# Retention, soft mixture and top-2 mixture on one core: a token table laid out by partition, and expert one's row list made from its own 24 columns

## The chip, the cores and the metric

One core of one Trainium2 chip. The metric is the device time of one execution, in microseconds. Three runs of the kernel before took 586.41, 589.7 and 592.46 us, so the median is 589.7.

## The reference, cut to what matters

```python
y = retention(q, k, v)                      # B, H, S, D = 4, 8, 768, 64
x = y.transpose(0, 2, 1, 3).reshape(3072, 512)
logits = x @ phi                            # soft mixture: 32 slots, 4 for each of 8 experts
d = softmax(logits, axis=0)                 # each slot over all tokens
slot_out = [relu((d.T @ x)[e] @ w1[e]) @ w2[e] for e in range(8)]
c = softmax(logits, axis=1)                 # each token over the 32 slots
x = c @ slot_out
noisy = x @ w_gate + log1p(exp(x @ w_noise)) * noise
top2 = two largest of noisy for each token, with their softmax as weights
for e in range(8):                          # w1: 512 x 1024, w2: 1024 x 512
    rows = tokens with e among their top2
    out[rows] += weight[rows] * (relu(x[rows] @ w1[e]) @ w2[e])
```

## The kernel before, in words

The first 195 us or so compute the retention and the soft mixture's slots. Its result `x` is never stored. A token's row of `x` is its 32 combine weights times the slot outputs, so for the second mixture the kernel keeps a small DRAM table, `ctab`: for each of the 3072 tokens 32 combine weights (`cs`, made in combine(), L561 to 577) and 8 gate weights (`wsl`, L689 to 692), 40 numbers of 4 bytes, in the order of the tokens, and a row of zeros behind them (L175). A hidden row of expert e is then the token's 32 weights times `gs` of e, which is the slot outputs times w1[e], made by g_dot(e) (`pg`), rounded into two parts (`gr`) and spread over the partitions (`gs`), by matmul for expert 0 (g_rep, L726) and by 16 small transfers on SyncE's queue for the others (g_copy, L737).

Gating (L633 to 692): on VectorE the two largest entries are picked (`sel`), `selh` marks both, and two steps of matmuls (`pt`, `pp`) count, for each token and expert, the token's place in the expert's list. `blk` (L676) is the block of 128 that the place lies in, `rr` (L677) the place within the block, for all 8 experts × 24 chunks of tokens = 192 columns; `cnt` (L679, ScalarE) the experts' counts. While VectorE and GpSimd do that, TensorE runs dummy matmuls (fill, tile `pw`; F4 of them before g_dot(0), L638).

lists(e) (L750) makes the list of an expert: `bm` (VectorE, which block), `bt` (GpSimd, `bm` times two constants, "base" for the chunk and "tok" for the token), `oh` (VectorE, 3 compares of `tab` with `rr`), `pli` (TensorE, 24 small matmuls), and `lt` and `ls` (VectorE), the token numbers. Expert 0 and 1 have lists of their own; lists_all() (L774) makes those of the other six together, in pieces that are resumed after the output blocks in PACED (L958 ff.): `bma`, `rk`, `rs` and `rh` after block (0, 1), `oh` after (0, 2), `sb` (GpSimd, L804) and `bta` (VectorE, L807) after (0, 3), and the same again for the second choice after (0, 4), (0, 5) and (1, 0). A piece is tied to its block by a mark, a copy of one element of the block's `yo` on ScalarE into the tile that the piece will write.

The experts: fetch() (L845) gathers table rows by the list (GpSimd, an indirect DMA for each block, `cg`), turn() (L855) rounds and transposes them (`cts`, `st` on ScalarE and VectorE, `ptc` on TensorE, `cts` again), hidden() (L895) multiplies by `gs` (`phc`) and makes both parts of the result (`hhl`: L907 on ScalarE, L909 and L912 on VectorE), and main() (L921) multiplies by w2 in three passes (`pyc`, 24 matmuls for a block of 128 rows), scales to `yo` on ScalarE, and add_rows() (L917) scatters `yo` to `out` from GpSimd by the same list `ls`, adding up. An expert has 7 blocks, six of 128 rows and one of 64; more than that goes to a loop at the end that is not entered here. Weights w1 and w2 (`V1`, `V2`) come by SyncE's queue; ScalarE and VectorE split V2 into `wh` and `wl`. load_paced (L963) ties a piece of a weight to a block by a mark like the ones above (L957), and SyncE issues its transfers in the order of the program. The order on each engine is set by a scheduler that keeps the order of the source, adds the edges of after(), and moves what it can.

Of the kernel before, what the change touches and what calls it, by code (L numbers as in the profile page):

```python
# [105 lines left out]
def kernel(ctx: ExitStack, tc: tile.TileContext, q, k, v, phi, w1, w2,  # L106
# [641 lines left out]
    LS = {}  # L748

    def lists(e, pool, ps, nb):  # L750
        rv = rr.rearrange("p (e c) -> p e c", e=E)
        bv = blk.rearrange("p (c e) -> p c e", e=E)
        bm = pool.tile([P, NCH, nb], F16, name="bm", bufs=1)
        nc.vector.tensor_tensor(bm, bv[:, :, e:e + 1].to_broadcast([P, NCH, nb]),
                                col16("iotab")[:, None, :nb].to_broadcast([P, NCH, nb]), op=OP.is_equal)
        bt = pool.tile([P, NCH, 2, nb], F16, name="bt", bufs=1)
        nc.gpsimd.tensor_tensor(bt[:, :, 0, :], bm, col16("base")[:, :, None].to_broadcast([P, NCH, nb]), op=OP.mult)
        nc.gpsimd.tensor_tensor(bt[:, :, 1, :], bm, col16("tok")[:, :, None].to_broadcast([P, NCH, nb]), op=OP.mult)
        oh = pool.tile([P, NCH // 8, P, 8], F16, name="oh", bufs=1)
        for c in range(NCH // 8):  # L760
            nc.vector.tensor_tensor(oh[:, c], tab, rv[:, e, None, 8 * c:8 * c + 8].to_broadcast([P, P, 8]),
                                    op=OP.is_equal)
        pl = ps.tile([P, 2, nb], F32, name="pli", tag="pt")
        for c in range(NCH):
# [354 lines left out]
```

## Time and profile before

| what | value |
|---|---|
| median of 3 runs | 589.7 us |
| profiled execution, its own time | 592.0 us |
| its span | 590.2 us |
| TensorE busy | 554.7 us, 94% of the span |
| VectorE, ScalarE, GpSimd busy | 43%, 41%, 38% |
| mean granted clock of TensorE | 0.964 |

The profiled execution took 2.3 us more than the median, and 1.8 us of it lie outside the span. The clock row of the page is full (9 of 10 or more) in nearly all slices behind the fifteenth, which is the stretch from about 215 us on.

### The profile page before, as it was taken

The page shows a single profiled execution, that of the slowest core. Times are in us where ns is not written, and L with a number is a line of the kernel's source. Part 1 is how long each engine was busy: PE and PEld are TensorE (multiplying, and loading weights), DVE is VectorE, ACT ScalarE, POOL GpSimd, SP SyncE. Part 2 cuts the span into 40 slices and gives each one's busy share as a digit, 9 for nine tenths or more (in the row PEclk, how much of TensorE's full clock was granted, in tenths as well). Part 3 has the DMA queues.
Part 4 walks back from the last instruction along what each step waited for, and adds up shares of the span by engine and source line. Part 5 has one row for each costly group of instructions (what it writes and reads, how often), then busy time and mean ns, then how long its engine had stood idle before and what let it go on. Part 6 is the DMA issues. An engine that isn't in the chain of part 4 may idle for free. (4 is left out here: it accounts for less than half of the span.)

```text
span 590.2 us, 10723 instructions
## 1 busy us (share of the span) xinstructions
PE 554.7 (94%) x4196; PEld 421.8 (71%) x4196; DVE 255.3 (43%) x529; ACT 243.7 (41%) x543; POOL 222.5 (38%) x214
## 2 busy tenths in 40 slices
PE   7999999999899878979999999999999999999990
PEld 4787888787443436858787787787787787788880
DVE  3566777764202366456625235235235234334200
ACT  2555656553101235245246246246345335335210
POOL 3524534330103055642455444344344436332231
PEclk7899999999699789989999999999999999999997
DMA  9999999998799942465446646656656644553232
GB/s 218 286 270 306 299 328 281 308 405 364 291 404 389 367 124 67 102 179 151 108 98 182 125 132 186 124 151 168 137 140 170 143 112 65 132 105 46 37 43 31
DMA packets 79485, 111.76 MB, mean 189 GB/s; under 512 B 10066, under 2 KB 51602, under 8 KB 78530
## 3 DMA queue, kind: packets, MB, share of 16 engines
q1 hardware_dynamic: 65808, 95.96, 49.3%
q0 software_dynamic: 9696, 14.37, 16.7%
q10 hardware_dynamic: 3922, 0.66, 0.6%
q8 instruction: 35, 0.57, 0.4%
q14 instruction: 24, 0.20, 0.1%
HBM read 87.92 MB, written 20.41 MB: 184 GB/s over the span
## 5 line engine op out<-in xcount | busy, mean ns | idle before, releaser
L937 PE MATMUL pyc<-wh,hhl 128*128 128x512 f32 x384 | 154.6, 403 | 0.2 <-ACT hhl L907 0.2
L938 PE MATMUL pyc<-wl,hhl 128*128 128x512 f32 x384 | 152.1, 396 | 0.0
L939 PE MATMUL pyc<-wh,hhl 128*128 128x512 f32 x384 | 151.5, 395 | 0.0
L918 POOL DMA_INDIRECT out_dram<-yo,lsa x42 | 66.1, 1575 | 136.1 <-ACT w L957 31.6
L909 DVE SCALAR_TENSOR_TENSOR hhl<-phc,hhl 128x512 fp32r<-128x512 f32 (+1 forms) x128 | 66.9, 551 | 84.9 <-ACT hhl L907 84.5
L939 PEld LDWEIGHTS pyc<-wh,hhl 128*128 128x128 f32 x384 | 72.6, 189 | 16.6
L937 PEld LDWEIGHTS pyc<-wh,hhl 128*128 128x128 f32 x384 | 72.1, 188 | 16.1 <-ACT hhl L907 0.4
L946 ACT ACTIVATE yo<-pyc,cg 128x512 f32<-128x512 f32 x48 | 33.0, 688 | 121.0 <-PE pyc L939 108.1
L938 PEld LDWEIGHTS pyc<-wl,hhl 128*128 128x128 f32 x384 | 72.4, 189 | 14.6
L907 ACT ACTIVATE hhl<-phc 128x512 fp32r<-128x512 f32 (+1 forms) x128 | 59.5, 513 | 8.0 <-PE phc L904 6.6
L885 DVE TENSOR_TENSOR wl<-w,wh 128x1024 fp32r<-128x1024 f32 x32 | 39.1, 1225 | 49.6 <-ACT wh L879 49.6
L851 POOL DMA_INDIRECT cg<-ctab,lsa x42 | 43.8, 1042 | 15.2 <-issue 14.9
L879 ACT CAST wh<-w 128x1024 fp32r<-128x1024 f32 x32 | 33.4, 1047 | 32.3 <-DMA w<-in_moe_w_dram 24.7
L298 DVE TENSOR_TENSOR am<-pa,cta 128x512 f32<-128x512 f32 x48 | 33.1, 692 | 28.6 <-PE py L322 15.3
L918 POOL DMA_INDIRECT out_dram<-yo,ls x14 | 25.0, 1787 | 47.4 <-ACT w L957 16.2
L256 POOL TENSOR_TENSOR comp<-raws,cta 64x512 f32<-64x512 f32 x24 | 24.9, 1039 | 40.7 <-PE py L322 16.5
L276 DVE TENSOR_TENSOR qT<-pt,cta 64x512 f32<-64x512 f32 x48 | 33.0, 688 | 16.6 <-PE pt L271 16.2
L256 POOL TENSOR_TENSOR vl<-raws,cta 64x512 f32<-64x512 f32 x24 | 24.9, 1038 | 33.5 <-PE py L322 22.6
L904 PE MATMUL phc<-cts,gs 128*128 128x256 f32 (+1 forms) x192 | 36.5, 299 | 0.5 <-ACT cts L873 0.5
L904 PEld LDWEIGHTS phc<-cts,gs 128*128 128x128 f32 x192 | 29.8, 191 | 7.3 <-issue 2.5
L294 PE MATMUL pa<-qT,kT 64*128 64x128 f32 x384 | 31.7, 296 | 0.7 <-DVE qT L276 0.7
L294 PEld LDWEIGHTS pa<-qT,kT 64*128 64x128 f32 x384 | 27.0, 198 | 5.2 <-issue 3.7
(195 smaller groups left out, 701.6 us busy)
## 6 DMA issues: line engine op xcount, KB each, us to landing
w<-in_moe_w_dram SPq DMA_DIRECT2D x80, 512.0 KB, 5.1
w<-in_moe_w_dram SPq DMA_DIRECT2D x11, 2048.0 KB, 10.5
comp<-in_q_dram SPq DMA_DIRECT2D x12, 512.0 KB, 6.7
out_dram<-zt SPq DMA_DIRECT2D x6, 1024.0 KB, 9.8
raws<-in_k_dram SPq DMA_DIRECT2D x11, 512.0 KB, 5.6
raws<-in_v_dram SPq DMA_DIRECT2D x11, 512.0 KB, 7.8
gs<-gr SPq DMA_DIRECT2D x112, 32.0 KB, 2.3
w<-in_moe_w_dram SPq DMA_DIRECT2D x2, 1024.0 KB, 21.1
```

Source lines behind the costliest of these rows:

```text
L256: pool_ins[0] = nc.gpsimd.tensor_tensor(VL[j][rs], RAW[u][1][gs, :, r, :], gv[gs, r, t, :, None].to_broadcast([64, H, D]), op=OP.mult)
L294: mm = nc.tensor.matmul(pa[s][:, hp, :], KT[j][r, hp, :], QT[t][r, hp, g, :], start=True, stop=True)
L851: nc.gpsimd.indirect_dma_start(out=cg[:rows(b), i, :], out_offset=None, in_=ctab, in_offset=index(e, b, rows(b)))
L879: ins = nc.scalar.copy(wh, V2[e][:, 1024 * i:1024 * i + 1024])
L885: nc.vector.tensor_tensor(wl, V2[e][:, 1024 * i:1024 * i + 1024], WH[e][i], op=OP.subtract)
L904: nc.tensor.matmul(ph[:, w * i:w * i + w], GS[e][:, kf + i], CT[e, g][:, :w], start=True, stop=True)
L907: relu.append(nc.scalar.activation(h[:, :, :w], pv, AF.Relu))
L909: last = nc.vector.scalar_tensor_tensor(h[:, :, w + t0:w + t0 + 2 * P], pv[:, :, :2 * P], 0.0, h[:, :, :2 * P], op0=OP.max, op1=OP.subtract)
L918: nc.gpsimd.indirect_dma_start(out=out, out_offset=index(e, b, n), in_=y, in_offset=None, bounds_check=N - 1, oob_is_err=False, compute_op ...
L937: nc.tensor.matmul(py, hhl[:, kf, ts], wh, start=(kf == 0), stop=False)
L938: nc.tensor.matmul(py, hhl[:, kf, ts], wl, start=False, stop=False)
L939: nc.tensor.matmul(py, hhl[:, kf, tl], wh, start=False, stop=(kf == KF - 1))
```

## The change

- **Table.** `ctab` is laid out by partition: row p·24 + c holds the token on partition p of chunk c. The combine weights and the gate weights live in one tile, `row` (128 × 24 × 40), which one transfer of ScalarE's queue writes (128 pieces of 3840 bytes). Gone are GpSimd's two transfers of `cs`, ScalarE's two of `wsl`, and the row of zeros. GpSimd's products of the gate weights now write into `row` (every fortieth to eighth column). combine_t() makes 24 matmuls of 32 columns where it had 6 transposes.
- **Lists.** As a table row is no longer a token number, places() makes two lists: `lg`, for the gather, in two steps on VectorE, and behind it `ls`, for the scatter, in three.
- **Expert 0's list** is issued right behind `blk`, on `r0`, the place within the block for its own 24 columns. `rr` for all 192 stands behind `lg`, g_dot(1) behind the list's last matmul.
- **Dummies.** F4 is 14 instead of 26; F5 = 6 stand behind g_dot(0). The reciprocal of the gate weights stands behind `selh`.
- **Weights and gates.** All four pieces of V1[2] are loaded at once (one waited for a copy on GpSimd, L994). The two halves of the first gates are split one at a time. g_copy(2) comes at block 3 (hook (0, 3, 5)) instead of block 0 (hook (0, 0, 6)).
- **Later lists.** `sb` in lists_all() gets a mark, like `bta`.

```diff
-F1, F2, F3, F4 = 2, 0, 0, 26
+F1, F2, F3, F4, F5 = 2, 0, 0, 14, 6
...
-    cols["tok"] = tok[:, None]
+    cols["row"] = j[:, None]
...
-    ctab = tc.dram_tile([N + 1, NS + E], F32, name="ctab")
+    ctab = tc.dram_tile([N, NS + E], F32, name="ctab")
...
+    def places(pool, pl, shape, sfx=""):
+        lt, la = (pool.tile(shape, F32, name=n + sfx, bufs=1) for n in ("lt", "la"))
+        lg, ls = (pool.tile(shape, I32, name=n + sfx, bufs=1 if sfx else None) for n in ("lg", "ls"))
+        nc.vector.tensor_scalar(lt, pl[:, 0], 1.0 / C, float(NCH), op0=OP.mult, op1=OP.add)
+        ins = nc.vector.scalar_tensor_tensor(lg, pl[:, 1], float(NCH), lt, op0=OP.mult, op1=OP.add)
+        with after(ins):
+            nc.vector.tensor_scalar(la, pl[:, 1], 64.0, -127.0, op0=OP.is_ge, op1=OP.mult)
+            nc.vector.scalar_tensor_tensor(la, pl[:, 1], 2.0, la, op0=OP.mult, op1=OP.add)
+            nc.vector.scalar_tensor_tensor(ls, lt, float(C), la, op0=OP.mult, op1=OP.add)
+        return ins, lg, ls
...
-            for r in range(2):
-                nc.gpsimd.dma_start(row_view(r)[:, :, :NS], cs[64 * r:64 * r + 64])
...
-                    nc.tensor.transpose(pc[:, g, :], cs[:, a:a + 4].rearrange("p i s -> p (i s)"), ident)
+                    for q in range(4):
+                        nc.tensor.matmul(pc[32 * q:32 * q + 32, g, :], cs[:, a + q], ident, start=True, stop=True,
+                                         skip_group_check=True)
...
-            g_dot(0, pgd[0])
+            mm = g_dot(0, pgd[0])
+        with after(mm):
+            fill(psB, "pw", F5, 1)
...
-        g_dot(1, pgd[1])
...
-        nc.vector.tensor_tensor(rr.rearrange("p (e c) -> p c e", e=E), pp[:, :NCH * E].rearrange("p (c e) -> p c e", e=E),
-                                blk.rearrange("p (c e) -> p c e", e=E), op=OP.subtract)
+        pv, bv = (t[:, :NCH * E].rearrange("p (c e) -> p c e", e=E) for t in (pp, blk))
+        r0 = small.tile([P, NCH], F16, name="r0")
+        nc.vector.tensor_tensor(r0, pv[:, :, 0], bv[:, :, 0], op=OP.subtract)
+        l0 = lists(0, small, psB, LB, late, r0)
+        with after(l0[0]):
+            g_dot(1, pgd[1])
+        with after(l0[1]):
+            nc.vector.tensor_tensor(rr.rearrange("p (e c) -> p c e", e=E), pv, bv, op=OP.subtract)
         nc.scalar.copy(cnt, pp[0:1, NCH * E:])
...
-        for r in range(2):
-            put = nc.scalar.dma_start(row_view(r)[:, :, NS:], wsl[64 * r:64 * r + 64])
+        put = nc.scalar.dma_start(ctab.rearrange("(p c) s -> p c s", p=P), row)
...
-        for i in range(KD - 1):
+        for i in range(KD):
             nc.sync.dma_start(V1[2][:, 1024 * i:1024 * i + 1024], v1p[:, i])
...
-            for a, name in enumerate(("base", "tok")):
+            for a, name in enumerate(("base", "row")):
+                mark(sb[0:1, a, 0, 0:1], y)
                 nc.gpsimd.tensor_tensor(sb[:, a], sels[i], col16(name)[:, :, None].to_broadcast([P, NCH, E]),
                                         op=OP.mult)
...
+    with after(l0[0]):
+        gr0 = cc.tile([P, 2, 2, QF], F32R, name="gr2", bufs=1)
         for i in range(2):
-            his.append(nc.scalar.copy(pgs[:, QF * i:QF * i + QF], pgd[i]))
-    with after(his[3], *lists(0, cc, psC, LB)):
-        gr0 = g_split(pgs, 2)
-        g_rep(0, gr0, 0)
+            nc.scalar.copy(pgs[:, QF * i:QF * i + QF], pgd[i])
+            nc.scalar.copy(gr0[:, 0, i], pgs[:, QF * i:QF * i + QF])
+            last = nc.vector.tensor_tensor(gr0[:, 1, i], pgs[:, QF * i:QF * i + QF], gr0[:, 0, i], op=OP.subtract)
+            if i == 0:
+                g_rep(0, gr0, 0)
+                his = [split_hi(0, i) for i in range(2)]
...
-            nc.gpsimd.tensor_copy(V1[2][0:1, 3072:3073], cg0[0:1, 0, 0:1])
-            nc.sync.dma_start(V1[2][:, 3072:], v1p[:, 3])
...
-        g_copy(2, g_split(pg2, 1), 0)
-
+        gr2.append(g_split(pg2, 1))
+
+    gr2 = []
     HOOK[0, 0, 6] = g_rest,
+    HOOK[0, 3, 5] = (lambda: g_copy(2, gr2[0], 0)),
```

The order of VectorE behind `pp`, before:

```order
L676 TENSOR_SCALAR blk<-pp 128x192
L677 TENSOR_TENSOR rr<-pp,blk 128x24x8
L710 CAST identr<-ct 128x128
L714 TENSOR_SCALAR pselr<-ct 128x64 x4
L754 TENSOR_TENSOR bm<-blk,ct_80 128x168
L761 TENSOR_TENSOR oh<-tab,rr 128x1024 x3
L768 TENSOR_SCALAR lt<-pli 128x7
L770 TENSOR_TENSOR ls<-lt,pli 128x7
```

And after; `r_2456` is the tile `r0`:

```order
L708 TENSOR_SCALAR blk<-pp 128x192
L711 TENSOR_TENSOR r_2456<-pp,blk 128x24
L221 TENSOR_TENSOR bm<-blk,ct_80 128x168
L228 TENSOR_TENSOR oh<-tab,r_2456 128x1024 x3
L208 TENSOR_SCALAR lt<-pli 128x7
L209 SCALAR_TENSOR_TENSOR lg<-pli,lt 128x7
L211 TENSOR_SCALAR la<-pli 128x7
L716 TENSOR_TENSOR rr<-pp,blk 128x24x8
L212 SCALAR_TENSOR_TENSOR la<-pli,la 128x7
L213 SCALAR_TENSOR_TENSOR ls<-lt,la 128x7
L748 CAST identr<-ct 128x128
L752 TENSOR_SCALAR pselr<-ct 128x64 x4
```

`rr` has moved from the place behind `blk` to one behind `lg`, and the two constants for the transposes (`identr`, `pselr`) behind the list.

ScalarE between the first two blocks of expert 0, before; the `w` copies are marks of a weight's piece, `bma` and `rk` marks of a list's:

```order
L946 ACTIVATE yo<-pyc,cg 128x512
L957 COPY w<-yo 1x1
L946 ACTIVATE yo<-pyc,cg 128x512
L907 ACTIVATE hhl<-phc 128x320
L777 CAST bma<-yo 1x1
L777 CAST rk<-yo 1x1
L957 COPY w<-yo 1x1
L907 ACTIVATE hhl<-phc 128x320 x6
L879 CAST wh<-w 128x1024
L907 ACTIVATE hhl<-phc 128x320
L946 ACTIVATE yo<-pyc,cg 128x512
```

And after:

```order
L956 ACTIVATE yo<-pyc,cg 128x512
L967 COPY w<-yo 1x1
L883 COPY cts<-ptc 128x320
L889 CAST wh<-w 128x1024
L956 ACTIVATE yo<-pyc,cg 128x512
L917 ACTIVATE hhl<-phc 128x320
L789 CAST bma<-yo 1x1
L789 CAST rk<-yo 1x1
L967 COPY w<-yo 1x1
L917 ACTIVATE hhl<-phc 128x320 x7
L873 CAST cts<-cg 128x96
```

The rounding `wh` of the first piece of V2[1] stood behind the second `yo`, and seven of `hhl`; now it stands ahead of that `yo`.

GpSimd from the first gather of expert 0 to the second `sb` pair, before (`out_dram` rows are the scatters):

```order
L804 TENSOR_TENSOR sb<-sel_2422,ct_80 128x192 x2
L757 TENSOR_TENSOR bt<-bm,ct_80 128x24x7
L758 TENSOR_TENSOR bt<-bm,ct_80 128x24x7
L851 DMA cg<-ctab,ls 128x40 x4
...
L918 DMA out_dram<-yo,ls 3072x512
L851 DMA cg<-ctab,ls 128x40 x2
L918 DMA out_dram<-yo,ls 3072x512 x3
L849 MEMSET cg 64x40
L804 TENSOR_TENSOR sb<-sel_2430,ct_80 128x192 x2
L918 DMA out_dram<-yo,ls 3072x512 x5
```

And after:

```order
L224 TENSOR_TENSOR bt<-bm,ct_80 128x24x7
L225 TENSOR_TENSOR bt<-bm,ct_80 128x24x7
L861 DMA cg<-ctab,lg 128x40 x4
...
L928 DMA out_dram<-yo,ls 3072x512
L861 DMA cg<-ctab,lg 128x40 x2
L928 DMA out_dram<-yo,ls 3072x512 x3
L817 TENSOR_TENSOR sb<-sel_2429,ct_80 128x192 x2
L859 MEMSET cg 64x40
L928 DMA out_dram<-yo,ls 3072x512 x4
L817 TENSOR_TENSOR sb<-sel_2437,ct_80 128x192 x2
L928 DMA out_dram<-yo,ls 3072x512
```

The first `sb` pair stood ahead of `bt` of expert 0; it now stands behind the fourth scatter, and the second pair four scatters later. On SyncE, 16 + 8 `gs` transfers stand ahead of the first piece of V2[1] where 16 + 16 stood.

## Rows read from the trace of the kernel before

**Rows 1.** Stretches: per engine busy us (instructions); then granted clock, DMA share, GB/s.
```profile
217.00:220.00 3.00, 3.00 (x11) 0.96 (x10) 2.95 (x5) 0.00 (x0) 2.07 (x2) 0.50 0.12 30
...
257.75:260.00 2.25, 2.25 (x7) 1.78 (x8) 0.06 (x1) 0.43 (x1) 0.00 (x0) 0.52 0.85 154
260.00:263.00 3.00, 3.00 (x13) 2.36 (x13) 1.92 (x3) 2.42 (x10) 1.40 (x1) 0.79 0.14 31
263.00:576.00 313.00, 313.00 (x1592) 249.42 (x1591) 118.20 (x245) 132.36 (x297) 128.24 (x102) 1.00 0.54 124
```

**Rows 2.** Waits of TensorE, 190 to 280 us: total us, times, longest.
```profile
PE pli L765 <- POOL bt L758: 4.3, 2, 3.5
PE ptc L870 <- DVE st L865: 3.7, 1, 3.7
```

**Rows 3.** Timeline of TensorE: start, us, instruction, count, idle before it.
```profile
183.53 0.85 PE L584 MATMUL pcn<-ct,cs 128*128 128x128 f32 x6
...
202.70 4.30 PE L144 MATMUL pw<-ones 128*128 128x512 f16 x18
...
215.37 1.57 PE L765 MATMUL pli<-bt,oh 128*128 128x14 f16 x24 [3.45 <-POOL bt L758]
...
224.06 0.97 PE L904 MATMUL phc<-cts,gs 128*128 128x256 f32 x6 [0.46 <-ACT cts L873]
...
266.02 0.31 PE L904 MATMUL phc<-cts,gs 128*128 128x320 f32 x1
...
290.09 1.68 PE L812 MATMUL pli<-bta,oh 128*128 128x112 f16 x24
```

**Rows 4.** Timeline of SyncE's queue (issues only).
```profile
228.18 18.97 SPq L741 DMA_DIRECT2D gs<-gr  x29
247.25 14.96 SPq L958 DMA_DIRECT2D w<-in_moe_w_dram  x5
```

**Rows 5.** Timeline of ScalarE.
```profile
211.61 0.15 ACT L679 COPY cnt<-pp 1x8 f32<-1x8 f32 x1 [1.13 <-DVE rr L677]
...
222.55 0.24 ACT L863 CAST cts<-cg 128x64 fp32r<-128x64 f32 x1
...
242.19 0.69 ACT L946 ACTIVATE yo<-pyc,cg 128x512 f32<-128x512 f32 x1 [4.18 <-PE pyc L939]
...
252.43 1.05 ACT L879 CAST wh<-w 128x1024 fp32r<-128x1024 f32 x1 [4.06 <-DMA w<-in_moe_w_dram]
```

**Rows 6.** Timeline of VectorE.
```profile
210.49 1.04 DVE L677 TENSOR_TENSOR rr<-pp,blk 128x192 f16<-128x192 f32 x1
...
212.05 2.51 DVE L761 TENSOR_TENSOR oh<-tab,rr 128x1024 f16<-128x1024 f16 x3
...
261.42 3.02 DVE L807 TENSOR_TENSOR bta<-bma,sb 128x1344 f16<-128x1344 f16 x2
...
286.25 3.03 DVE L807 TENSOR_TENSOR bta<-bma,sb 128x1344 f16<-128x1344 f16 x2 [2.04 <-ACT bta L777]
```

**Rows 7.** Timeline of GpSimd.
```profile
212.03 1.98 POOL L804 TENSOR_TENSOR sb<-sel,ct 128x192 f16<-128x192 f16 x2 [3.36 <-PE pg L185]
...
217.63 1.91 POOL L851 DMA_INDIRECT cg<-ctab,ls  x1 [2.31 <-DVE ls L770]
...
246.25 1.62 POOL L918 DMA_INDIRECT out_dram<-yo,ls  x1 [0.30 <-issue]
...
261.60 2.81 POOL L918 DMA_INDIRECT out_dram<-yo,ls  x1 [4.62 <-ACT w L957]
...
264.66 0.97 POOL L804 TENSOR_TENSOR sb<-sel,ct 128x192 f16<-128x192 f16 x2
```

**Rows 8.** Scatters into `out` (ns), their landing (us), and `ctab`'s (last column, us).
```profile
L918 POOL DMA_INDIRECT out_dram<-yo,ls x9: 1424/1616/2815, 240.6 to 293.0; - x9
...
DMA to landing us min/median/max: 2.5/5.4/8.2
...
ctab<-cs POOLq DMA_DIRECT2D x2, 192.0 KB, 8.0
```

More of the change, by code (lines that the diff above doesn't have):

```diff
@@ L206, in load_w, with lists @@
         store[e] = t
+    LS, LG = {}, {}
+    def places(pool, pl, shape, sfx=""):
[8 more added lines that the diff above has]
+        return ins, lg, ls
+    def lists(e, pool, ps, nb, keep=None, rv=None):
+        if rv is None:
+            rv = rr.rearrange("p (e c) -> p e c", e=E)[:, e]
+        bv = blk.rearrange("p (c e) -> p c e", e=E)
+        bm = pool.tile([P, NCH, nb], F16, name="bm", bufs=1)
+        nc.vector.tensor_tensor(bm, bv[:, :, e:e + 1].to_broadcast([P, NCH, nb]),
+                                col16("iotab")[:, None, :nb].to_broadcast([P, NCH, nb]), op=OP.is_equal)
+        bt = pool.tile([P, NCH, 2, nb], F16, name="bt", bufs=1)
+        nc.gpsimd.tensor_tensor(bt[:, :, 0, :], bm, col16("base")[:, :, None].to_broadcast([P, NCH, nb]), op=OP.mult)
+        nc.gpsimd.tensor_tensor(bt[:, :, 1, :], bm, col16("row")[:, :, None].to_broadcast([P, NCH, nb]), op=OP.mult)
+        oh = pool.tile([P, NCH // 8, P, 8], F16, name="oh", bufs=1)
+        for c in range(NCH // 8):
+            nc.vector.tensor_tensor(oh[:, c], tab, rv[:, None, 8 * c:8 * c + 8].to_broadcast([P, P, 8]),
+                                    op=OP.is_equal)
+        pl = ps.tile([P, 2, nb], F32, name="pli", tag="pt")
+        for c in range(NCH):
+            mm = nc.tensor.matmul(pl.rearrange("p a b -> p (a b)"), oh[:, c // 8, :, c % 8], bt[:, c].rearrange("p a b -> p (a b)"),
+                             start=(c == 0), stop=(c == NCH - 1))
+        last = places(keep or pool, pl, [P, nb])
+        LG[e], LS[e] = last[1:]
+        return mm, last[0]
     bctx = ExitStack()
@@ L494 @@
         blk = late.tile([P, NCH * E], F16, name="blk")
-        wsl = late.tile([P, NCH, E], F32, name="wsl")
+        row = late.tile([P, NCH, NS + E], F32, name="row")
+        wsl = row[:, :, NS:]
         cnt = late.tile([1, E], F32, name="cnt")
@@ L556 @@
         nc.vector.transpose(ht[2].rearrange("p j s -> p (j s)"), hs.rearrange("p j s -> p (j s)"))
-        cs = small.tile([P, NCH, NS], F32, name="cs")
+        cs = row[:, :, :NS]
         mx, sm = (small.tile([P, NCH], F32, name=n) for n in ("mx", "sm"))
@@ L662 @@
         selh = small.tile([P, NCH * E], F16, name="selh")
-        nc.vector.tensor_add(selh, sels[0].rearrange("p c e -> p (c e)"), sels[1].rearrange("p c e -> p (c e)"))
+        both = nc.vector.tensor_add(selh, sels[0].rearrange("p c e -> p (c e)"), sels[1].rearrange("p c e -> p (c e)"))
         tc_h = small.tile([P, 2, P], F16, name="tc_h")
@@ L684 @@
         nc.gpsimd.tensor_scalar(w[:, 1], w[:, 0], 1.0, 1e-9, op0=OP.add, op1=OP.add)
-        nc.vector.reciprocal(w[:, 1], w[:, 1])
+        with after(both):
+            nc.vector.reciprocal(w[:, 1], w[:, 1])
         nc.gpsimd.tensor_tensor(w[:, 2], w[:, 0], w[:, 1], op=OP.mult)
@@ L746, in g_one @@
         g_copy(e, g_split(pg, 1), 0)
[L748 to L764, printed above, removed]
-            mm = nc.tensor.matmul(pl.rearrange("p a b -> p (a b)"), oh[:, c // 8, :, c % 8], bt[:, c].rearrange("p a b -> p (a b)"),
-                             start=(c == 0), stop=(c == NCH - 1))
-        lt = pool.tile([P, nb], F32, name="lt", bufs=1)
-        nc.vector.tensor_scalar_add(lt, pl[:, 0, :], float(N))
-        ls = pool.tile([P, nb], I32, name="ls")
-        last = nc.vector.tensor_tensor(ls, lt, pl[:, 1, :], op=OP.add)
-        LS[e] = ls
-        return mm, last
     def lists_all():
@@ L816, in lists_all @@
                 y = yield
-        lt = cc.tile([P, E, LB], F32, name="lta", bufs=1)
-        nc.vector.tensor_scalar_add(lt, pl[:, 0], float(N))
-        ls = cc.tile([P, E, LB], I32, name="lsa", bufs=1)
-        nc.vector.tensor_tensor(ls, lt, pl[:, 1], op=OP.add)
+        lg, ls = places(cc, pl, [P, E, LB], "a")[1:]
         for e in range(2, E):
-            LS[e] = ls[:, e]
+            LG[e], LS[e] = lg[:, e], ls[:, e]
         for g in range(G):
@@ L976 @@
     pgs = cc.tile([P, DM], F32, name="yt", bufs=1)
-    his = [split_hi(0, i) for i in range(2)]
-    with after(his[1]):
+    with after(l0[0]):
+        gr0 = cc.tile([P, 2, 2, QF], F32R, name="gr2", bufs=1)
         for i in range(2):
-            his.append(nc.scalar.copy(pgs[:, QF * i:QF * i + QF], pgd[i]))
-    with after(his[3], *lists(0, cc, psC, LB)):
-        gr0 = g_split(pgs, 2)
-        g_rep(0, gr0, 0)
+            nc.scalar.copy(pgs[:, QF * i:QF * i + QF], pgd[i])
[4 more added lines that the diff above has]
+                his = [split_hi(0, i) for i in range(2)]
+    with after(his[1], l0[1]):
         pg2 = psC.tile([P, QF], F32, name="pg", tag="phc", bufs=4)
@@ L987 @@
         fetch(0, 0)
-        cg0 = CG[0, 0]
         ga = turn(0, 0)
```

19 lines of the change are left out of this document (8 added, 11 removed).

## The prediction

> **What bounds the kernel now.** I read the page first: TensorE is busy for most of the span. Then the table of stretches: from 263 to 576 us it is busy for 313.00 of 313.00 us at a granted clock of 1.00 [rows 1]. So after that point time can be won only by shifting the whole stretch, and a new wait there is paid in full. Next the list of waits of TensorE between 190 and 280 us: two entries of weight, 4.3 us (two waits, the longer 3.5) for GpSimd's `bt` of the row lists, and 3.7 us at `ptc` for VectorE's `st` [rows 2]. Behind both the clock shows half speed: 0.50 in 217 to 220, and after the second 0.52 in 257.75 to 260 and 0.79 in 260 to 263 [rows 1]. The second fall costs 2.25 × 0.48 + 3.0 × 0.21 = 1.7 us. Last the timelines around these places. The first expert's list ends in `pli` at 215.37; the first hidden matmul, `phc`, starts at 224.06 [rows 3], and from there TensorE hardly stops but for the 3.7 us. Those come from afar: SyncE spends 18.97 us on 29 small `gs` transfers from 228.18 and issues the second weight only at 247.25 [rows 4]; ScalarE waits 4.06 us for it and converts at 252.43 [rows 5], and everything behind that on ScalarE and VectorE, `st` included, is late.
>
> Sums are made against the profiled execution, 592.0 us (span 590.2, 1.8 outside it, taken as unchanged). It lies 2.3 above the median of 589.7, so 2.3 comes off at the end. About 1% of the time, 5.9 us, is what a measurement can tell from no change.
>
> **Term a: the start of the experts, up to the first hidden matmul.** Twelve dummies fewer stand ahead of g_dot(0) and six are put behind it. 18 took 4.30, or 0.24 each [rows 3], so `pt`, behind all of them, comes 12 × 0.24 − 6 × 0.24 = 1.4 earlier; the reciprocal that moves behind `selh` keeps that input from being later. The 24 transposes that take the place of 6 have between no cost (four narrow ones side by side) and 24 × 0.85/6 − 0.85 = 2.6 (none so) [rows 3]; I take 0.6 of it, as given back by the half microsecond for which TensorE waits for the last soft-MoE weight: with the two software transfers of `cs` gone that weight has less beside it. Both ends stay in the range.
>
> Behind `pp`, VectorE made `rr` from 210.49 (1.04) and two constants before `bm` and `oh` [rows 6]. Now it makes 24 columns from about 210.49 − 1.4 = 209.1 and `bm` is there at 209.8. On GpSimd the two `sb` (1.98) are gone from in front of `bt`; the products of `bt` took from 214.0, the end of `sb`, to `pli` at 215.37, or 1.4 [rows 3, 7], and I allow 1.6 beside `oh`. So `pli` begins at about 211.5 instead of 215.37, and the first gather, as far behind it as before, at 213.7 instead of 217.63: 3.9 earlier.
>
> This lead is mostly eaten. `rr` now runs behind `pli`, `lt`, `lg` and `la`, so until about 214.7. ScalarE's `cnt` waits for it by the program's order of waits, as in the trace, where `cnt` starts 0.08 behind `rr` [rows 5, 6]. Behind `cnt` in ScalarE's queue stand the copies `yt`, the rounding of the first weights, `gr` and `gs`: 3.1 later than 211.61. The halves of expert one's gate are now copied and sent one by one, which wins some of that back: summing the queue's durations I get `cts` at 219.9, not 222.55 [rows 5]. The gather alone would allow 213.7 + (222.55 − 217.63) = 218.6. A weight's rounding (1.05) now stands between `cts` and `st`, and from `cts` to `phc` took 1.5. So `phc` starts at about 219.9 + 1.5 + 1.0 = 222.4: −1.7. Bounds: −3.9 if all of the list's lead survives; +1.0 if the new table transfer is late (a rival below). One table transfer replaces three kinds; GpSimd's longer strided products delay it to about 209.5, and it must land by 213.7.
>
> **Term b: the second weight.** The fourth piece of V1[2] no longer waits for a copy on GpSimd, and only 24 `gs` transfers stand before V2[1] instead of 32, since g_copy(2)'s second half comes later. At 18.97/29 = 0.65 each from 220.1 the weight is issued at 235.9 instead of 247.25, and with its 5.2 us (247.25 to 252.43) it is there at 241.1 [rows 4, 5]. The wait of 3.7 goes, and the 1.7 of clock with it: −5.4 (bounds −3.7, if the clock falls for another reason, and −5.4).
>
> **Term c: a new wait in its place.** On ScalarE the rounding of this weight now stands ahead of `yo` of the second block, and `wl` (VectorE) ahead of that block's followers. That `yo` would start at 242.19 − 1.7 = 240.5 [rows 5]; it now starts at 241.1 + 1.05 = 242.15, 1.65 late, and VectorE adds its `wl` of 1.2, of which about half lies beside the rest. The hidden matmul of the next expert that needs these buffers comes 2.2 late. Bounds 0 (the landing 2 us sooner) and 4.0 (as long as today's wait). I take +2.2.
>
> **Term d: GpSimd's `sb` of the later lists.** Before, its first pair ran at 212.03, hoisted. Now a mark ties it to `yo` of the fourth block, and in GpSimd's order it stands behind the fourth scatter, which waits for that `yo` and, by the program, for the landing of the scatter before. VectorE's two `bta` wait for it, and behind them on VectorE a step `hhl` of the next expert's hidden rows, for which TensorE waits. The scatter began at 261.60 [rows 7]; with a, b up to there (3.7 + 1.1 of the clock) and c it begins at 261.60 − 1.7 − 4.8 + 2.2 = 257.3. Then 1.6 for itself (median [rows 8]), 0.2, `sb` 0.49 [rows 7], two `bta` 3.0 [rows 6], `hhl` 0.6, and some 0.3 of signals: 263.5. TensorE would be there at 266.02 − 1.7 − 5.4 + 2.2 = 261.1 [rows 3]. So +2.4; bounds 0, and +7.4 if the scatter before lands late.
>
> The row shows that beside VectorE's compares and products GpSimd is slow: `sb` 1.98 at 212.03 against 0.97 at 264.66, and a scatter of 2.81 beside `bta` against 1.6 [rows 7, 8]. The Trainium skill, SBUF — State Buffer, section "SBUF: two separate sides", says that the two engines share one pair of ports, held by one of them for a whole instruction. The trace agrees with it. By that rule the scatter here, with `bta` now waiting, keeps to 1.6; were it held as at 261.60, term d would be 1.2 more.
>
> **Term e: the second pair.** `bta` of the second pair started at 286.25, before the scatter of the same block could matter, and ended 0.8 before `pli` at 290.09 [rows 3, 6]. Now scatter (1.6), `sb` (0.49) and some 0.6 of signals come first: 2.7 − 0.8 = +1.9, bounds 0 and 3.
>
> The list's added VectorE steps (0.2 each), the extra gate copy and the split halves lie beside TensorE's busy time once it is full; if that cover goes they cost less than 1. The overflow path isn't run.
>
> Sum: −1.7 − 5.4 + 2.2 + 2.4 + 1.9 = −0.6, so 591.4 on the profiled execution and **589.1** against the median: no change that can be measured. The gain at 254 us is real but handed back at three smaller waits.
>
> **Rivals.**
> 1. The waits c, d and e don't bind: the weight lands a little sooner and `sb` comes before TensorE needs it. For it: each is under 2.5 us, of the size of the errors in my replay; against: all three add links to chains that were tight. −0.6 − 6.5 = −7.1, or 589.1 − 6.5 = 582.6: faster.
> 2. The waits bind and the clock falls behind them. For: both idles of 3.5 and 3.7 were followed by half clock; against: the new ones, 1.9 to 2.4, are shorter than either. Each fall costs 1.7, so two or three make 592.5 to 594.2. The Trainium skill, TensorE: Matmul & The Clock Gate, "HAM oscillation — how this bites in real kernels", describes such waits throwing the clock back again and again; the two falls here agree with it, and fewer dummies speak the same way.
> 3. The table comes late. The `cs` half took 8.0 to land [rows 8]. One table transfer that took as long from 209.5 would hold the first gather to 217.6; `phc` then starts at 225.1 and not 222.4: +2.7, 591.8. Against: it goes from ScalarE's queue, in long pieces, when the queues are nearly empty.
> 4. Slower: the scatters' chain. Each waits for the one before to land, median 5.4 and longest 8.2 [rows 8]. The second stands at 246.25 [rows 7], and its `yo` ends no later than before. At 8.2 each the fourth begins not at 257.3 but at about 246 + 8.2 + 8.2 = 262.4, with `sb`, `bta` and TensorE behind: +5.1 and a fall of the clock, 1.7, so 589.1 + 6.8 = 595.9. It decides once that scatter begins later than 262. For: it is a new dependence of TensorE on scatters; against: the median is far shorter.
>
> **How the numbers follow.** Forecast (589.1, own range 586.5 to 591.5) 0.38; rival 1 0.22, of which 0.02 stays within 1%; rival 2 0.20; rival 3 0.08; rival 4 0.12. Faster by over 1% 0.20, within 1% 0.38 + 0.02 + 0.20 + 0.08 = 0.68, slower 0.12. The range runs from rival 1 to the far end of rival 2, 582.5 to 594.5.
>
> **What would show it.** First `phc` near 222.4 with `cnt` behind `rr` near 214.7 (a); no idle of 3.7 at `ptc`, and the second weight issued near 236 (b); a stop of about 2 near 244 (c); TensorE stopped near 261 to 263 with `sb` behind the fourth scatter (d), and again at `pli` near 286 (e). The forecast is wrong if the gaps c to e are missing (rival 1), if granted clock is 0.5 behind them (rival 2), if the first gather stands idle for the table (rival 3), or if the fourth scatter starts past 262 (rival 4).

## The result, and the profile after

The changed kernel took 596.18 us (median of 4 runs, 593.52 to 597.31), the kernel before beside it 590.75 (4 runs, 586.41 to 592.46). The ratio is 1.0113, with a 95% interval from 1.007 to 1.0156: slower by a little over 1%, and above the stated range. The profiled execution took 597.31 us with a span of 595.4, so it compares with 592.0 and 590.2 before: 5.2 us more in the span. Here and below a median is over all runs, while a ratio and its interval leave out the runs that lie more than 1.5% above the fastest of their kernel (8 of 29 of the kernel before on one chip, 594.31 to 597.13 us; 3 of 6 in one of the experiments).

The waits of TensorE from 180 to 330 us (total us, times, longest), to be read beside [rows 2]:

```profile
PE phc L914 <- DVE hhl L922: 3.8, 2, 2.9
...
PE pli L825 <- DVE bta L820: 2.4, 1, 2.4
PE phc L914 <- ACT cts L883: 1.8, 1, 1.8
```

The wait for `st` of 3.7 is gone. In its place stand a wait of 2.9 at `phc` for `hhl` (with a smaller one of 0.9 the sum is 3.8), one of 2.4 at the later lists' `pli`, one of 1.8 at the first `phc`. These are terms d, c, e and a of the forecast.

The stretches (busy us and instructions of TensorE, its weight loads, VectorE, ScalarE, GpSimd; then granted clock, DMA share, GB/s), beside [rows 1]:

```profile
212.00:221.00 9.00, 8.38 (x78) 4.28 (x81) 6.62 (x16) 5.25 (x13) 5.11 (x6) 0.50 0.76 250
...
227.00:240.00 13.00, 12.16 (x71) 9.12 (x70) 9.17 (x23) 5.69 (x15) 4.29 (x5) 0.87 0.19 45
...
266.00:270.00 4.00, 1.88 (x9) 1.65 (x10) 4.00 (x13) 1.35 (x4) 0.00 (x0) 0.93 0.65 178
270.00:280.00 10.00, 10.00 (x58) 8.12 (x57) 4.27 (x11) 3.78 (x10) 3.03 (x2) 0.86 0.22 59
...
290.00:300.00 10.00, 7.61 (x46) 6.04 (x45) 6.45 (x10) 1.85 (x4) 4.75 (x4) 0.84 0.46 118
```

Half clock for nine microseconds ahead of the first hidden matmul, and three more falls: 0.87 of 227 to 240, 0.93 and 0.86 of 266 to 280 behind the wait near 268, and 0.84 of 290 to 300, around the wait near 296. They cost 13 × 0.13 = 1.7, 4 × 0.07 + 10 × 0.14 = 1.7 and 10 × 0.16 = 1.6 us, where before there was the one behind 257.75 (1.7). The nearest idle of note ahead of the fall in 227 to 240 is one of 0.84 us, and the forecast has no term for that fall.

TensorE's timeline, beside [rows 3]: the transposes, g_dot(1), the first `phc`, and the three stops behind it.

```profile
185.14 1.52 PE L614 MATMUL pcn<-ct,row 128*32 128x128 f32 x48
...
213.47 3.64 PE L179 MATMUL pg<-w,sotT 128*32 128x256 f32 x32
...
225.91 0.98 PE L914 MATMUL phc<-cts,gs 128*128 128x256 f32 x6 [1.84 <-ACT cts L883]
...
250.16 0.38 PE L914 MATMUL phc<-cts,gs 128*128 128x320 f32 x1 [0.89 <-DVE hhl L922]
...
268.12 0.39 PE L914 MATMUL phc<-cts,gs 128*128 128x320 f32 x1 [2.90 <-DVE hhl L922]
...
296.15 2.09 PE L825 MATMUL pli<-bta,oh 128*128 128x112 f16 x24 [2.39 <-DVE bta L820]
```

The transposes took 1.52 and not 0.85, 0.67 more. g_dot(1) took 3.64 at half clock. SyncE's queue, beside [rows 4]:

```profile
240.76 0.39 SPq L968 DMA_DIRECT2D w<-in_moe_w_dram  x1
241.25 4.95 SPq L779 DMA_DIRECT2D gs<-gr  x8
```

ScalarE beside [rows 5], then VectorE beside [rows 6], then GpSimd beside [rows 7]:

```profile
215.05 0.16 ACT L717 COPY cnt<-pp 1x8 f32<-1x8 f32 x1 [4.46 <-DVE la L212]
...
220.96 0.29 ACT L873 CAST cts<-cg 128x64 fp32r<-128x64 f32 x1
...
225.48 0.37 ACT L883 CAST cts<-ptc 128x256 fp32r<-128x256 f32 x1 [3.10 <-PE pw L144]
...
245.38 1.05 ACT L889 CAST wh<-w 128x1024 fp32r<-128x1024 f32 x1 [3.89 <-issue]
246.34 0.68 ACT L956 ACTIVATE yo<-pyc,cg 128x512 f32<-128x512 f32 x1
```

```profile
264.18 3.32 DVE L820 TENSOR_TENSOR bta<-bma,sb 128x1344 f16<-128x1344 f16 x2 [2.93 <-POOL sb L817]
267.43 0.41 DVE L919 SCALAR_TENSOR_TENSOR hhl<-phc,hhl 128x256 fp32r<-128x256 f32 x1
```

```profile
214.79 1.09 POOL L861 DMA_INDIRECT cg<-ctab,lg  x1 [2.88 <-DVE la L211]
...
262.05 1.55 POOL L928 DMA_INDIRECT out_dram<-yo,ls  x1 [3.95 <-ACT hhl L917]
263.05 1.56 POOL L817 TENSOR_TENSOR sb<-sel,ct 128x192 f16<-128x192 f16 x2
```

Ahead of the fourth scatter GpSimd's queue waited, from 256.3 us for 5.06 us, behind the issue of the third scatter at 256.42:

```profile
L928 POOLq EVENT_SEMAPHORE  x1: 5059/5059/5059, 256.3 to 256.3; - x1
```

`cnt` waits for VectorE to 215.05, as forecast; `cts` starts at 220.96 (219.9 forecast). The rounding `wh` of the second weight starts at 245.38, ahead of the second `yo` at 246.34. `sb` stands behind the fourth scatter (262.05 + 1.55 and the pair's 1.56 overlap in the records), `bta` (3.32) behind `sb`, and the `hhl` steps behind `bta`; TensorE goes on at 268.12. The fourth `yo` (259.65, 0.69 long) was done at 260.34, so the last of the queue's wait, to 261.3, was not for it: the semaphore waited for is the one that the third scatter's landing raises.

The way from before to after, from landmarks that both traces have (TensorE's `pst` at the end of the soft mixture, the first `phc`, and ScalarE's full-block `yo`):

| stretch | before | after | difference |
|---|---|---|---|
| start to `pst` | 194.41 | 196.42 | +2.0 |
| `pst` to first `phc` | 29.65 | 29.49 | −0.2 |
| first `phc` to fourth `yo` | 35.97 | 33.74 | −2.2 |
| fourth to fifth `yo` | 12.86 | 16.73 | +3.9 |
| fifth to eighth `yo` | 23.18 | 27.10 | +3.9 |
| eighth `yo` to TensorE's end | 280.84 | 280.57 | −0.3 |
| TensorE's end to the span's end | 13.3 | 11.35 | −1.9 |

The 7.8 us of the fourth and fifth rows are more than the whole difference of 5.2. The third row holds the gain of the second weight (3.7 of wait and the 1.1 of clock that lay before the fourth `yo`), less the wait of 0.89 and the fall of 1.7 in 227 to 240.

### The profile page after: what moved, and what is told of

The parts are those of the page before. It is cut to its first block, busy times and chain, and to the rows that moved or that the text cites. A ratio compares the mean times of both kernels' runs of the same rounds, so it can differ in the third digit from the quotient of the medians.

```text
span 595.4 us, 10802 instructions
## 1 busy us (share of the span) xinstructions
PE 556.8 (94%) x4232; PEld 423.7 (71%) x4232; DVE 257.1 (43%) x539; ACT 244.3 (41%) x548; POOL 214.8 (36%) x211
## 5 line engine op out<-in xcount | busy, mean ns | idle before, releaser
L861 POOL DMA_INDIRECT cg<-ctab,lga x42 | 41.1, 979 | 24.6 <-issue 22.3
L928 POOL DMA_INDIRECT out_dram<-yo,ls x14 | 23.4, 1669 | 48.6 <-DVE yo L961 11.8
```

Of the source, the lines that this page charges most:

```text
L861: nc.gpsimd.indirect_dma_start(out=cg[:rows(b), i, :], out_offset=None, in_=ctab, in_offset=index(LG, e, b, rows(b)))
L928: nc.gpsimd.indirect_dma_start(out=out, out_offset=index(LS, e, b, n), in_=y, in_offset=None, bounds_check=N - 1, oob_is_err=False, comput ...
```

## The experiments

Theory M: the two marks on `sb` put TensorE behind the scatters' queue on GpSimd, and each wait costs its length and mostly a fall of the clock. Theory S, the rival: the loss lies ahead of the first hidden matmul, in the half clock from 212 to 221 us and in ScalarE's queue behind `rr`. Runs that were sent together share a chip and the runs of the kernel before; a ratio is always against those.

**Without the marks on sb.**

```diff
             for a, name in enumerate(("base", "row")):
-                mark(sb[0:1, a, 0, 0:1], y)
```

> The changed kernel without the two marks on sb; nothing else differs, and in GpSimd's order the first sb pair then stands behind the seven gathers of expert 0, long before the fourth scatter. Theory M (the marks put TensorE behind the scatters): the idles of 2.90 us at phc near 268 and 2.39 at pli near 296 go, and the half clock behind each with them, so about 7.8 us less than the changed kernel, near 588.4 us, some 2 below before. Theory S (the loss lies ahead of the first hidden matmul, in the half clock from 212 to 221 and ScalarE's queue): the idles may go but the time stays within 2 us of the changed kernel's.

Measured: 584.68 us (12 runs) against 591.95 before on the same chip, ratio 0.991 (0.9878 to 0.9942). GpSimd's timeline shows `sb` at 224.70, before any scatter, and TensorE's clock is full from 240 us on:

```profile
224.70 0.97 POOL L816 TENSOR_TENSOR sb<-sel,ct 128x192 f16<-128x192 f16 x2
...
258.29 1.94 POOL L927 DMA_INDIRECT out_dram<-yo,ls  x1 [3.98 <-ACT hhl L916]
260.49 0.97 POOL L816 TENSOR_TENSOR sb<-sel,ct 128x192 f16<-128x192 f16 x2
```

```profile
260.00:265.00 5.00, 5.00 (x42) 4.24 (x41) 4.85 (x19) 3.04 (x8) 1.33 (x4) 1.00 0.89 275
...
290.00:300.00 10.00, 10.00 (x49) 8.21 (x48) 3.13 (x6) 4.86 (x13) 7.75 (x8) 1.00 0.27 66
```

Fourth to fifth `yo` takes 12.30 us here and fifth to eighth 23.18, against 16.73 and 27.10. The half clock from 212 to 221 is still there (g_dot(1) takes 3.64). The changed kernel, repeated on the same chip (below), took 590.93, so the two marks cost 6.2 us. Theory S is out as the cause of these; the kernel without marks is faster than before.

**The kernel before with the marks.**

```diff
+                mark(sb[0:1, a, 0, 0:1], y)
                 nc.gpsimd.tensor_tensor(sb[:, a], sels[i], col16(name)[:, :, None].to_broadcast([P, NCH, E]),
```

> The kernel before with the two marks on sb added, nothing else; its sb pairs then stand behind the fourth and the eighth scatter. Theory M: two idles of 2 to 3 us appear near 266 and 292 and clock falls follow, so 5 to 8 us slower than before, near 597. Theory S: within 2 us of before.

Measured: 597.54 (6 runs) against 591.95, ratio 1.0124 (1.0065 to 1.0184). Its waits:

```profile
PE phc L905 <- DVE hhl L913: 3.4, 1, 3.4
...
PE pli L813 <- DVE bta L808: 2.4, 1, 2.4
PE ptc L871 <- DVE st L866: 1.9, 1, 1.9
```

Both waits are there, 3.4 and 2.4, in a kernel that has nothing else of the change; fourth to fifth `yo` takes 18.15 and fifth to eighth 27.09. M holds from the other side. The 3.7 at `ptc` shrank to 1.9, and with `sb` gone from in front of `bt` the first `phc` came 26.90 behind `pst`, not 29.65.

**g_dot(1) ahead of the list.**

```diff
         nc.tensor.matmul(pp[:, :NCH * E], trih, selh, start=False, stop=True)
+        g_dot(1, pgd[1])
...
-        with after(l0[0]):
-            g_dot(1, pgd[1])
```

> The changed kernel with g_dot(1) back right behind pp, ahead of the list's matmuls, so TensorE works 1.9 us in the wait for bt. Theory S: the clock stays at full speed from 212 to 221, g_dot(1) takes 1.9 and not 3.6, and the first hidden matmul comes 2 us or more sooner, near 594 us. Theory M: the first hidden matmul may move by a microsecond, the idles near 268 and 296 stay, so 595 to 596 us.

Measured: 590.93 (12 runs) against 591.95, ratio 1.0002 (0.9964 to 1.0039). This run told nothing of what it was made for: the scheduler put g_dot(1) back behind the list, and the order on all five engines is that of the changed kernel, row for row. So it is a repeat of the changed kernel, and it did not show the 596.

**cnt on VectorE.**

```diff
-        nc.scalar.copy(cnt, pp[0:1, NCH * E:])
+        nc.vector.tensor_copy(cnt, pp[0:1, NCH * E:])
```

> The changed kernel with the copy cnt on VectorE instead of ScalarE, so ScalarE's queue no longer waits for rr. If that wait held the first hidden matmul: ScalarE's yt and wh start near 212 instead of 215.1 and phc comes 1 to 2 us sooner, near 594.5. If something else held it (the half clock of TensorE, the late transposes): phc within 0.5 us of 225.9 and the time unchanged.

Measured: 590.67 (12 runs) against 591.95, ratio 1.0015 (0.9976 to 1.0054): level with the repeat above. ScalarE's timeline:

```profile
207.51 0.36 ACT L990 COPY yt<-pg 128x256 f32<-128x256 f32 x1
...
214.23 0.37 ACT L990 COPY yt<-pg 128x256 f32<-128x256 f32 x1 [4.16 <-PE pg L179]
```

ScalarE did start earlier, and then waited 4.16 us for g_dot(1), which ran at half clock. From `pst` to `phc` it took 26.72, against 26.54 in the repeat. `cnt` is a wait that another one covers.

**The changed kernel again.**

> The changed kernel itself once more, beside the others. Theory M: 6 to 8 us above the kernel without the marks, with idles of 2.9 and 2.4 at the same two places and a clock fall behind each; against before it then lies between 591 (as the row-for-row equal kernel with g_dot(1) moved in the source) and 596 us. Rival P (the 596 of the first four runs was a property of the program): near 596 again, clear of before.

Measured: 591.12 (12 runs) against 589.84 before on the same chip, ratio 1.0035 (1.0002 to 1.0067). Rival P is out: 596 is not a fixed property of the program. On that chip the changed kernel is some 6 us above the kernel without its marks (with ten more dummies, below) and the one with its weight part alone. This profile (span 586.7) has the waits, 2.3, 2.4 and 1.7, but only one fall:

```profile
243.38 0.38 PE L914 MATMUL phc<-cts,gs 128*128 128x320 f32 x1 [2.34 <-DVE hhl L922]
...
262.45 0.38 PE L914 MATMUL phc<-cts,gs 128*128 128x320 f32 x1 [2.44 <-DVE hhl L922]
```

```profile
240.00:245.00 5.00, 2.66 (x11) 1.88 (x10) 5.00 (x14) 2.21 (x9) 3.89 (x3) 0.92 0.46 137
245.00:250.00 5.00, 5.00 (x18) 4.06 (x18) 2.95 (x10) 3.00 (x12) 0.96 (x2) 0.74 0.41 54
...
260.00:270.00 10.00, 7.57 (x53) 6.38 (x53) 6.34 (x19) 2.68 (x7) 1.47 (x1) 1.00 0.39 100
270.00:280.00 10.00, 10.00 (x49) 8.25 (x49) 8.42 (x13) 6.68 (x16) 3.12 (x2) 1.00 0.53 137
```

The clock falls behind the wait of 2.34 (0.92 of 240 to 245 and 0.74 of 245 to 250, 1.7 us in all) and not behind the one of 2.44, nor behind the 1.7. Fourth to fifth `yo` takes 14.91 and fifth to eighth 25.01, so the marks cost 2.6 and 1.8 here, against 4.4 and 3.9 in the first profile.

**The weight part alone, on the kernel before.**

```diff
...
-        for i in range(KD - 1):
+        for i in range(KD):
             nc.sync.dma_start(V1[2][:, 1024 * i:1024 * i + 1024], v1p[:, i])
...
-            nc.gpsimd.tensor_copy(V1[2][0:1, 3072:3073], cg0[0:1, 0, 0:1])
-            nc.sync.dma_start(V1[2][:, 3072:], v1p[:, 3])
...
-        g_copy(2, g_split(pg2, 1), 0)
+        gr2.append(g_split(pg2, 1))
...
+    HOOK[0, 3, 5] = (lambda: g_copy(2, gr2[0], 0)),
```

> The kernel before with only the weight part: all four pieces of V1[2] at once, no copy on GpSimd, g_copy(2) at block 3. If term b is the gain: the idle of 3.7 at ptc near 254 and the half clock behind it go, a wait of about 1 comes near 246, so 4 to 5 us below before. If the gain of the kernel without marks comes from the earlier list instead: less than 1.5 us.

Measured: 584.91 (12 runs) against 589.84, ratio 0.9922 (0.9891 to 0.9952), some 4.6 us. SyncE's queue, and the one wait that is left near the second weight:

```profile
211.13 17.02 SPq L741 DMA_DIRECT2D gs<-gr  x26
233.36 0.39 SPq L958 DMA_DIRECT2D w<-in_moe_w_dram  x1
```

```profile
242.97 0.39 PE L904 MATMUL phc<-cts,gs 128*128 128x320 f32 x1 [0.69 <-DVE rh L793]
```

The second weight is issued at 233.36 behind 26 `gs` transfers, not behind 32, and its wait at TensorE is 0.69 where 3.7 stood. The 26 transfers end at 228.15; what holds the weight now is the mark of the first `yo` (232.42). Term b is the change's gain, and nearly all of it: the kernel without marks (0.991) has the earlier list as well and is no faster than this one (0.9922) within the intervals.

**Dummies behind pp, without the marks**, and then **with cnt on VectorE as well**.

```diff
-        nc.tensor.matmul(pp[:, :NCH * E], trih, selh, start=False, stop=True)
+        mm = nc.tensor.matmul(pp[:, :NCH * E], trih, selh, start=False, stop=True)
+        with after(mm):
+            fill(psB, "pw", 10, 1)
...
-        nc.scalar.copy(cnt, pp[0:1, NCH * E:])
+        nc.vector.tensor_copy(cnt, pp[0:1, NCH * E:])
```

> The kernel without the marks, with ten more dummies behind pp, in TensorE's wait for bt. If the half clock holds the first hidden matmul: granted clock 1.00 from 209 to 220, g_dot(1) in 1.9 and not 3.6 us, phc 1 us or more sooner counted from pst, time 1 to 2 us less. If ScalarE's queue holds it: the clock stays up, phc moves by under 0.5, and the time is the same within noise.

> The same with the copy cnt on VectorE, so that ScalarE's queue doesn't wait for rr. If clock and queue hold the first hidden matmul together: phc another 1 to 2 us sooner than with the dummies alone, and 2 to 4 us less than the kernel without marks. If the gather's landing or the table holds it: no change from the dummies alone.

Measured: with the dummies 585.28 (12 runs) against 589.84, ratio 0.9923 (0.9892 to 0.9955). The clock stays up and g_dot(1) takes 1.93:

```profile
204.40 2.32 PE L144 MATMUL pw<-ones 128*128 128x512 f16 x10
207.28 1.57 PE L232 MATMUL pli<-bt,oh 128*128 128x14 f16 x24 [0.57 <-POOL bt L225]
208.78 1.93 PE L179 MATMUL pg<-w,sotT 128*32 128x256 f32 x32
```

From `pst` to `phc` 26.18, against 27.34 in the kernel without marks; but kernels without these dummies have anything from 26.04 to 29.49, so this gain is not shown to be theirs. The second weight comes hardly sooner (issued 40.3 behind `pst`, against 40.7), the wait near 240 grows to 1.9, a fall follows it (0.83 of 240 to 250), and the time is the same. An earlier start is not worth anything while the next weight sets the pace. With `cnt` moved too: 588.69 (6 runs, from 580.43 to 591.42), ratio 0.9869 (0.9803 to 0.9935), which rests on three of the six; too scattered to tell from the one without. Its profile caught one slow gather on GpSimd, which made the first `cts` 3.0 us late:

```profile
216.29 4.48 POOL L862 DMA_INDIRECT cg<-ctab,lg  x1 [0.30 <-issue]
```

The other gathers of this list take 0.9 to 2.0. What held it is open.

**The first piece of the second weight earlier, without the marks.**

```diff
             g_copy(1, gr0, 1)
+            load_paced(V2, v2, 1, 0, (9, 1, 2, 3))
+            t, src, i = feed.pop((0, 9))[0]
+            nc.scalar.copy(t[0:1, 0, 0:1], HH[0, 0][0:1, 0, 0:1])
+            nc.sync.dma_start(t[:, :KF // 4], src[:, :KF // 4])
...
-            pre[0] += [(load_paced, V2, v2, e + 1, e, (0, SB, 1, 2) if e else (0, 1, 2, 3))]
+            pre[0] += [(load_paced, V2, v2, e + 1, e, (0, SB, 1, 2))] if e else []
```

> The kernel without the marks on sb, with the first piece of V2[1] issued behind the first 16 gs transfers, on a mark of expert 0's hidden rows instead of its first yo. Theory M with term c: the weight lands before the second yo is due, the wait of 1 to 2.4 us at phc near 245 goes, and with it any clock fall there, so 1.5 to 3 us below the kernel without marks, near 582 to 583. If that wait is hidden anyway: no change.

Measured: 583.23 (6 runs) against 591.06, ratio 0.9877 (0.983 to 0.9925). SyncE's queue and ScalarE's rounding:

```profile
217.26 11.27 SPq L779 DMA_DIRECT2D gs<-gr  x16
228.62 0.53 SPq L1018 DMA_DIRECT2D w<-in_moe_w_dram  x1
```

```profile
232.63 1.05 ACT L888 CAST wh<-w 128x1024 fp32r<-128x1024 f32 x1 [1.49 <-DMA w<-in_moe_w_dram]
```

The piece is issued behind 16 `gs` transfers and rounded before the first `yo` is due. No wait at `phc` for `hhl` is left in the list of waits, and the clock is 1.00 from 240 to 300. Term c was a real wait. No other kernel has a lower median; but the 2 us by which its ratio is below that of the kernel without marks (0.991) lie within the intervals, so what the early piece is worth in time is not shown.

**The marks one block earlier.**

```diff
-            y = yield
-            bt = cc.tile([P, NCH, 2, E, LB], F16, name="bta", bufs=1)
             sb = cc.tile([P, 2, NCH, E], F16, name="sb", bufs=1)
             for a, name in enumerate(("base", "row")):
                 mark(sb[0:1, a, 0, 0:1], y)
...
+            y = yield
+            bt = cc.tile([P, NCH, 2, E, LB], F16, name="bta", bufs=1)
+            for a in range(2):
                 mark(bt[0:1, 0, a, 0, 0:1], y)
```

> The changed kernel with both sb pairs made one piece earlier: marked by yo of the third and sixth block instead of the fourth and the seventh; as many marks as in the changed kernel. If the place behind the scatter of the same block is the cost: both idles go, 6 us below the changed kernel, level with the kernel without marks (near 585). If the marks themselves or sb on GpSimd at that time cost it: near 591.

Measured: 585.95 (9 runs) against 591.06, ratio 0.9902 (0.9869 to 0.9935). As many marks and the same `sb`, behind the third scatter instead of the fourth:

```profile
252.15 1.80 POOL L929 DMA_INDIRECT out_dram<-yo,ls  x1 [4.06 <-ACT cts L884]
253.42 1.54 POOL L815 TENSOR_TENSOR sb<-sel,ct 128x192 f16<-128x192 f16 x2
258.18 1.72 POOL L929 DMA_INDIRECT out_dram<-yo,ls  x1 [3.21 <-ACT hhl L918]
```

Both waits are gone. It is the place behind the scatter of the very block that the next step waits for, not the mark. An `sb` on the old mark but ahead of that scatter was not run, so the share of the scatter and its wait in the cost is read from the trace alone.

**The second mark alone.**

```diff
-                mark(sb[0:1, a, 0, 0:1], y)
+                if i:
+                    mark(sb[0:1, a, 0, 0:1], y)
```

> The changed kernel with the mark on the first sb pair left out and that on the second kept. Theory M, each mark on its own: the idle near 262 goes, the one of 1.7 to 2.4 at the second pli stays, with or without a clock fall: 2 to 4 us above the kernel without marks, near 588. If the second wait only came of the first: near 585.

Measured: 587.59 (12 runs) against 591.06, ratio 0.9948 (0.992 to 0.9977), between the kernel without marks and the changed one. The wait at the second `pli`, and the clock behind it:

```profile
PE pli L826 <- DVE bta L821: 3.0, 1, 3.0
```

```profile
290.00:300.00 10.00, 10.00 (x42) 8.20 (x42) 3.76 (x11) 2.84 (x7) 7.87 (x8) 0.85 0.37 111
```

3.0 us, and 10 × 0.15 = 1.5 of clock in this stretch: from the fifth to the eighth `yo` it takes 27.84, against 23.18. Each mark costs on its own.

## Why the prediction was wrong

By the first measurement it was wrong in size and in sign: no change was forecast, and slower by 1.1% came. Two repeats of the same instruction order gave 1.0002 (0.9964 to 1.0039) and 1.0035 (1.0002 to 1.0067), so the program as such is level with before or a few tenths of a per cent slower. What made the first four runs some 5 us slower than these is not shown. For the one that was profiled the stretches say where the time lies: its span is 5.6 us longer than that of the first repeat (595.4 against 589.8), 1.5 ahead of `pst`, 2.95 from there to the first `phc`, and 1.3 from there to the fourth `yo`, where it alone has a fall of the clock. Behind the fourth `yo` the two agree within 0.3.

**The step that failed** is the sum's treatment of the clock: "−1.7 − 5.4 + 2.2 + 2.4 + 1.9 = −0.6" prices the waits c, d and e by their length, and put the falls of the clock into a rival with 0.20. All three profiles of the changed order have falls behind the first `phc`: three in the first (one near 235, one each behind d and e), two in the first repeat (0.90 of 260 to 265 with 0.76 of 265 to 270, and 0.83 of 290 to 300), one behind c in the second. Each costs about 1.7 us, as the rival had it; the weight was wrong. The first profile's span changed by +5.2 and not by −0.6. Of these 5.8 us, 4.1 lie at d and e, and 3.3 of them are clock; 1.5 lie at a; the other stretches come to 0.2.

That the repeats came out near the forecast number is luck as far as the sum goes: there a won 3.1 and 3.4 instead of 1.7, and the last two stretches of the table were some 2 us shorter than in the profile of before, which about covered what the falls and the longer waits took.

The Trainium skill, TensorE: Matmul & The Clock Gate, "HAM oscillation — how this bites in real kernels", tells of a kernel whose waits between bursts of matmuls throw the clock back each time. The trace agrees for both long waits of before (3.45 and 3.72 us) and goes further than that case: here waits of 2.90 and 2.39 were followed by half clock too, and one of 2.44 was not.

Point by point:

- **Term a (−1.7)** went to pieces in the first profile and was exceeded in the others. In the first the `phc` came 29.49 behind `pst`, against 29.65. g_dot(1), which now stands behind the wait for `bt`, ran at half clock in all three (3.6 instead of 1.93); what differs in the first is that the clock stayed down longer (0.61 of 210 to 223, against 0.76 and 0.87 in the repeats), and a stop of 1.84 in which ScalarE's `cts` ran at 225.48 although `ptc` was done near 223.4. That stop is in one profile of three with this order; what caused it is open. In the repeats it was 26.54 and 26.30, so −3.1 and −3.4 against the profile of before. The reason given, that `cnt` holds ScalarE, wasn't borne out: with it taken away ScalarE waited for g_dot(1), at half clock, and the first `phc` came no sooner. "−3.9 if all of the list's lead survives" was nearly reached, for which the profile of before is partly to blame: its dummies took 7.72 partly at half clock, and with only the weight part changed it was 28.40. The half microsecond that was to give back 0.6 of the transposes' cost is no row of the trace of before; from the transposes to `pst` it took 11.28 with the change and 10.88, 11.20 and 11.11 in the three profiles with the code of before.
- **Term b (−5.4)** held: −4.6 in time with the weight part alone, with a small wait of 0.69 in it. The weight was issued at 240.76, 234.92 and 233.07 in the three profiles of the changed order (forecast 235.9). The 3.7 at `ptc` is in none of the profiles that have this part.
- **Term c (+2.2)**: 0.9, 1.1 and 2.3 in the three profiles. The weight waits for the mark of the first `yo` and for 24 `gs` transfers, which take 16.1 us. In the first profile the mark came last, in the second repeat, where expert 0 started earliest, the transfers did, and c was largest: what a wins, c can take. The run with the early first piece took it away.
- **Term d (+2.4)**: 2.9, 3.0 and 2.4. The chain, scatter, `sb`, `bta`, `hhl`, was right link by link, though the pair of `sb` took 1.56 behind the scatter in place of 0.49 for the first. Some 1.0 of it is the wait for the third scatter's landing (from the end of the `yo`, 260.34, to 261.3).
- **Term e (+1.9)**: 2.4, 2.4 and 1.7, and 3.0 with that mark alone.
- **Rival 1** (the waits don't bind) fell; its price was good, for with c, d and e all gone (the kernel with the early first piece) the ratio of 0.9877 is 7.3 us below before, where it adds up to −7.1. **Rival 3** (a late table) fell: where its landing is in the trace (four of the experiments) the table took 2.9 to 3.5 us, from an issue 4.8 to 5.0 ahead of the first gather. **Rival 4** was right in kind and wrong in size: the fourth scatter began at 262.05, past the 262 that it names, and had waited for the third to land, but that took 4.9 us from its start (256.42) and not 8.2, and cost the 1.0 given under d and not 5.1. Most of the 4.8 us by which it began later than the 257.3 of term d lie ahead of its `yo`.
- At most 0.4 of the 2.0 us ahead of `pst` are the change's (the transposes, under a): over the profiles `pst` lies between 191.57 and 196.42, and from 191.59 to 194.41 with the code of before in that part.

## What to carry to other kernels

A small product that only feeds another engine should not stand on a queue behind a transfer that waits for the very step which triggers both, and for the transfer before to land; one block earlier it cost nothing here. When a wait is taken out in one place and two short ones come in others, price the fall of TensorE's clock with each of them: in two of three profiles of the changed order the two falls made up 3.3 to 3.4 of the 8.4 us that the marks cost, in the third there was none. And an earlier start is worth only what the next late input leaves of it: in the kernels without the marks the second weight set the pace until its first piece was moved.
